# The first third of two units through the first layer during the last heads, and the denominator's product on GpSimd

## The chip, the core and the metric

The kernel runs on one core of one Trainium2 chip, as one launch. The metric is the device time in microseconds (us), taken as the median of several runs; a profile of one more execution comes with it. The engines are TensorE (PE, with its weight loads listed apart as PEld), VectorE (DVE), ScalarE (ACT) and GpSimd (POOL); SyncE (SP) issues the transfers.

## The reference

Three stages run one after the other, all in float32. The tensors q, k and v have 2 batches, 8 heads, 1152 rows and 64 columns.

```python
q_pool = q.reshape(B, H, S // 2, 2, D).mean(axis=3)
attn = softmax(q_pool @ k.T / sqrt(D)) @ v          # per head
x = attn as [1152 tokens, 512]

h = x @ w_in                                        # [1152, 2048]
P = a[0] + a[1]*h + a[2]*h**2 + a[3]*h**3
Q = 1.0 + abs(b[0])*abs(h) + abs(b[1])*h**2
x = (P / (Q + 1e-6)) @ w_out                        # [1152, 512]

xn = x / sqrt(mean(x*x) + 1e-6) * rms_g
out = (silu(xn @ w_gate) * (xn @ w_val)) @ w_out2   # width 1536
```

## The kernel before

**Work.** Every product of the two layers is three matmuls: activations and weights are kept as a high part and a low remainder, and high by high, high by low and low by high are summed in PSUM (`three`, line 507). Tokens are the columns, in NC = 3 thirds of CW = 384. A *unit* is 128 of the 2048 columns of the first layer, so there are 16 units; one unit takes 36 matmuls into its hidden tile `hid` (3 thirds, 4 slices kk of the 512 inputs, 3 products), and there are two such tiles in PSUM. Its function is computed from there, and 36 further matmuls take the result `g` into the sums `accp` of the second product, for a group of units at a time (GROUPS1 = 2, 4, 4, 4, 2).

**Attention.** 16 heads go in pairs, 9 tiles of 128 pooled rows to a pair, 72 tiles. Tiles are taken two by two: the scores (line 764), the row maximum `nm` on VectorE (793), the exponential `p` on ScalarE (799), the transposes on TensorE (815), their copies `pt` on ScalarE (847) or VectorE (850), and the product with v (`av`, 919). At the end of a pair of heads the copies `xt` are divided (970, 975) and split into x_hi and x_lo. The two score tiles are the same two PSUM tiles that the units use afterwards. Transposes of k, q and of the reciprocal sums (`rx`, 966) go through a PSUM tile of their own, `prep`. During attention the weights, which come as 64-bit numbers, are also decoded to float32 (`wc`) and split; what does not fit in SBUF goes to DRAM (`spill`, lines 211 to 232) and is fetched later. ScalarE, VectorE and GpSimd share that work.

**The function of a unit** (`rational`, line 1106 on, in `chain`). With u = m_u, p = m_p and q = m_q it is: u = |b1 h| (ACT 1106), p = a3 h + a2 (ACT 1109, all signs turned), p = p h (DVE 1112), p = (p + a1) h (DVE 1115), q = (u + b0) h (DVE 1122), q = |q| (ACT 1125), Ln and Exp of q for the reciprocal (ACT 1128, 1134), a correction factor from q and u (GpSimd 1140 after ACT 1131 for even units, DVE 1137 for odd ones), p = (p + a0) u (DVE 1143), g (DVE 1146), its high part (ACT 1154) and its low part (GpSimd 1157). Lines 1106, 1109, 1112, 1115 and 1122 read h from PSUM, and the hidden tile is free for the unit after next when they are done. Units 0 and 1 (FINE) do this third by third, the others for all tokens at once.

**Order.** Nothing is ordered by the engines. `Op` objects with an engine, a cost, a key and dependences are put in a list, and `order` sets each engine's queue once, while the program is built: of the operations that could start first by the costs, it takes the one with the smallest key. Some operations have several `ways`, that is engines, to choose from. What is written in the costs thus sets the order on the chip, and an engine works off its queue in that order, waiting where an input is not there. `order` runs once for attention (with `project_ops` of units 0 and 1 already in the list) and once for both layers.

## Time and profile before

| what | value |
|---|---|
| median of 3 runs | 723.6 us (721.89 to 726.38) |
| the profiled execution | 723.87 us |
| its span, first to last instruction | 722.0 us |
| mean granted TensorE clock | 0.986 of full speed |
| attention, until the first matmul of unit 0 | 265.15 us |
| busy: PE, DVE, ACT, POOL | 694.9, 542.4, 402.2, 299.7 us |

The times in the rows are counted from the start of the span. A row of a window gives the busy time of every engine in it, with the number of its instructions in brackets. A row of the chain gives start, length and work of a step of the path that ended last; "issue" there is time in which the profile shows nothing that the engine waited for. In a timeline, start and length of each instruction are followed by engine, line, and what it writes and reads.

### The profile page before, as it was taken

The page shows a single profiled execution, that of the slowest core. Times are in us where ns is not written, and L with a number is a line of the kernel's source. Part 1 is how long each engine was busy: PE and PEld are TensorE (multiplying, and loading weights), DVE is VectorE, ACT ScalarE, POOL GpSimd, SP SyncE. Part 2 cuts the span into 40 slices and gives each one's busy share as a digit, 9 for nine tenths or more (in the row PEclk, how much of TensorE's full clock was granted, in tenths as well). Part 3 has the DMA queues.
Part 4 walks back from the last instruction along what each step waited for, and adds up shares of the span by engine and source line. Part 5 has one row for each costly group of instructions (what it writes and reads, how often), then busy time and mean ns, then how long its engine had stood idle before and what let it go on. Part 6 is the DMA issues. An engine that isn't in the chain of part 4 may idle for free.

```text
span 722.0 us, 13129 instructions
## 1 busy us (share of the span) xinstructions
PE 694.9 (96%) x5257; PEld 605.0 (84%) x5257; DVE 542.4 (75%) x706; ACT 402.2 (56%) x620; POOL 299.7 (42%) x275
## 2 busy tenths in 40 slices
PE   7899999999999998899899999999999999999997
PEld 6677677767776777799899999998999899989996
DVE  4699988988888876887977879957769146945844
ACT  4668768778777767888755766435333223302210
POOL 4035546565655664424432343435345033513400
PEclk9999999999999999899999999999999999999999
DMA  6424536356554426114104104010223212420103
GB/s 208 118 76 150 154 99 216 128 186 220 167 183 162 145 108 233 59 59 145 59 30 146 59 0 147 26 35 0 88 88 119 87 58 70 136 88 29 59 1 131
DMA packets 51596, 77.13 MB, mean 107 GB/s; under 512 B 4176, under 2 KB 33872, under 8 KB 51536
## 3 DMA queue, kind: packets, MB, share of 16 engines
q1 hardware_dynamic: 51536, 76.30, 32.6%
q8 instruction: 41, 0.67, 0.4%
q14 instruction: 19, 0.16, 0.1%
HBM read 61.87 MB, written 14.42 MB: 106 GB/s over the span
## 4 chain that ended last, share of the span: by engine, by line
PE 88%; DVE 4%; ACT 4%; issue 1%; DMA 1%; SPq 0%; POOL 0%; POOLq 0%; DVEq 0%; ACTq 0%
PE hid L507 33%; PE accp L507 23%; PE hid L764 11%; PE av L919 10%; PE hid L815 7%; PE prep L712 3%; ACT p L799 2%; DVE nm L793 2%; ACT pt L847 1%; PE prep L966 1%; DMA wout_lo<-far 1%; DMA qn<-in_q_dram 1%; DVE win_lo L204 0%; ACT m_u L1106 0%; ACT m_q L1125 0%
## 5 line engine op out<-in xcount | busy, mean ns | idle before, releaser
L507 PE MATMUL hid<-x_hi,win_hi 128*128 128x384 f32 x480 | 162.7, 339 | 5.3 <-issue 2.8
L507 PE MATMUL hid<-x_lo,win_hi 128*128 128x384 f32 x480 | 161.8, 337 | 0.0
L507 PE MATMUL hid<-x_hi,win_lo 128*128 128x384 f32 x480 | 161.4, 336 | 0.0
L799 ACT ACTIVATE p<-hid,nm 128x1152 f32<-128x1152 f32 x72 | 88.0, 1222 | 36.8 <-DVE nm L793 36.6
L793 DVE TENSOR_REDUCE nm<-hid 128x1 f32<-128x1152 f32 x72 | 95.1, 1353 | 9.5 <-PE hid L764 8.8
L764 PE MATMUL hid<-kT,qT 64*128 64x256 f32 (+3 forms) x800 | 98.1, 379 | 0.6 <-ACT qT L598 0.2
L507 PEld LDWEIGHTS hid<-x_hi,win_hi 128*128 128x128 f32 x480 | 91.0, 190 | 8.0 <-issue 5.6
L507 PEld LDWEIGHTS hid<-x_lo,win_hi 128*128 128x128 f32 x480 | 91.0, 190 | 1.3 <-DVE x_lo L1315 0.3
L507 PEld LDWEIGHTS hid<-x_hi,win_lo 128*128 128x128 f32 x480 | 90.9, 189 | 0.0
L764 PEld LDWEIGHTS hid<-kT,qT 64*128 64x128 f32 (+1 forms) x800 | 73.6, 180 | 11.7 <-issue 1.6
L815 PEld LDWEIGHTS hid<-ident,p 64*128 64x128 f32 x1296 | 53.1, 141 | 33.5 <-ACT p L799 14.6
L919 PE MATMUL av<-pt,vn 128*64 128x288 f32 x576 | 76.7, 411 | 0.0
L815 PE MATMUL hid<-ident,p 64*128 64x64 f32 x1296 | 66.8, 231 | 9.0 <-ACT p L799 7.8
L1157 POOL TENSOR_TENSOR g_lo<-m_p,g_hi 128x1152 fp32r<-128x1152 f32 (+1 forms) x20 | 44.1, 2211 | 69.4 <-ACT g_hi L1154 69.4
L847 ACT ACTIVATE pt<-hid 128x512 f32<-128x512 f32 (+2 forms) x127 | 56.0, 477 | 25.3 <-PE hid L815 24.3
L507 PE MATMUL accp<-g_hi,wout_hi 128*128 128x384 f32 x192 | 66.0, 344 | 4.2 <-DVE acc L1212 2.0
L199 POOL TENSOR_SCALAR win_hi<-wc 128x512 fp32r<-128x512 f32 x26 | 18.2, 698 | 123.0 <-PE hid L507 104.1
L171 ACT ACTIVATE wc<-wraw 128x512 f32<-128x512 f32 x68 | 45.8, 675 | 41.7 <-POOL wout_lo L204 19.5
L850 DVE COPY pt<-hid 128x512 f32<-128x512 f32 (+2 forms) x97 | 50.9, 541 | 22.6 <-PE hid L815 21.1
L507 PE MATMUL accp<-g_lo,wout_hi 128*128 128x384 f32 x192 | 65.8, 343 | 0.6 <-POOL g_lo L1157 0.6
L507 PE MATMUL accp<-g_hi,wout_lo 128*128 128x384 f32 x192 | 65.7, 342 | 0.0
L919 PEld LDWEIGHTS av<-pt,vn 128*64 128x64 f32 x576 | 38.6, 136 | 26.9 <-issue 2.8
(118 smaller groups left out, 1276.0 us busy)
## 6 DMA issues: line engine op xcount, KB each, us to landing
wraw<-in_moe_w_out_dram SPq DMA_DIRECT2D x28, 512.0 KB, 3.4
far<-spill SPq DMA_DIRECT2D x23, 512.0 KB, 3.2
wraw<-in_moe_w_in_dram SPq DMA_DIRECT2D x16, 512.0 KB, 4.0
wraw<-in_moe_w_gate_dram SPq DMA_DIRECT2D x12, 512.0 KB, 3.6
wraw<-in_moe_w_val_dram SPq DMA_DIRECT2D x12, 512.0 KB, 3.7
kn<-in_k_dram SPq DMA_DIRECT2D x16, 288.0 KB, 3.7
vn<-in_v_dram SPq DMA_DIRECT2D x16, 288.0 KB, 3.4
qn<-in_q_dram SPq DMA_DIRECT2D x16, 256.0 KB, 3.4
```

The costliest lines, as they stand in the source:

```text
L171: nc.scalar.activation(c.bitcast(F32), wt["raw", n][:, :, 1].bitcast(F32), AF.Abs, scale=2.0**-112)
L199: eng.tensor_scalar(hi, w_float(n), 1.0, 1.0, op0=ALU.mult, op1=ALU.mult)
L507: ins = nc.tensor.matmul(dst, lhsT=a[x], rhs=b[y], start=first and i == 0 and p == 0, stop=last and i == n - 1 and p == 2,)
L712: seen(nc.tensor.transpose(ps[0:src.shape[1], at:at + 128], src, ident))
L764: ins = nc.tensor.matmul(ps[to, j, c:c + x1 - x0], lhsT=qT[2 * pr + h][rows, c0:c0 + to.stop - to.start], rhs=kT[2 * pr + h][rows, x0:x1], ...
L793: nc.vector.tensor_reduce(out=e["nm"], in_=scores(), op=ALU.max, axis=AX.X, negate=True)
L799: nc.scalar.activation(e["p"], scores(), AF.Exp, bias=e["nm"], scale=1.0, accum_out=sums[pr][:, t:t + 1])
L815: ins = nc.tensor.transpose(ps[:, g, c:c + 64], e["p"][rows, 128 * j:128 * j + 128], ident[rows, rows])
L847: return nc.scalar.activation(to, src, AF.Copy)
L850: return nc.vector.tensor_copy(to, src)
L919: nc.tensor.matmul(e["av", h][64 * c:64 * c + 64, 0:QW], lhsT=v_tile[2 * pr + h][:, KEYS[kt], :], rhs=pt[pr, h][:, kt, c * QW:(c + 1) * QW ...
L1157: eng.tensor_sub(g_(1), p_(), g_(0).bitcast(F32))
```

## The change

Two things are changed. First, for units 0 and 1 (PRE) the first third of the tokens, which belongs to the first batch and is ready long before the end of attention, is multiplied (12 matmuls a unit, into `prep`) and taken through the whole function while the last six of the 72 tiles run; the result stays in a new tile `pre`, and the buffers of k and of the pooled q serve as scratch. After attention only thirds 1 and 2 of these units are left, and `pre` is only split into its two parts. Secondly, for all 16 units the denominator is formed another way: ScalarE takes |h| without a factor, then w = b1 |h| + b0 (reading SBUF, in place of its |q|), and GpSimd multiplies w by |h|, in place of VectorE's line 1122. To make room, v has two buffers instead of three, and an unused constant goes.

```diff
     ON_POOL = range(0, 16, 2)
+    Q_POOL = range(16)
...
+        if w == "in" and u in PRE:
+            parts = [(c, kks) for c, kks in parts if c]
...
+    PRE = (0, 1)
+    def pre_ops(u, key, consts):
+        bps, bu, bq, bp = Buf("prep"), Buf("kn"), Buf("qp"), Buf("pre")
...
+        n = CW
+        mm = None
+        for kk in range(KC):
+            mm = Op(PE, cost(PE, 3 * n), key, lambda kk=kk: f_mm(kk), [mm or kq_mm[0], wop["in", u], *xop[0, kk]], [bps, *wbuf["in", u]])
+        o_abs = Op(ACT, cost(ACT, n), key + 2000, lambda: A(u_(), h_(), AF.Abs), [mm, *consts], [bps, bu])
+        o_p1 = Op(ACT, cost(ACT, n), key + 2000, lambda: A(p_(), h_(), AF.Identity, bias=na2, scale=na3), [mm, *consts], [bps, bp])
+        o_p2 = Op(DVE, cost(DVE, n), key + 2500, lambda: nc.vector.tensor_mul(p_(), p_(), h_()), [o_p1], [bps, bp])
+        o_p3 = Op(DVE, cost(DVE, n), key + 3000, lambda: stt(p_(), p_(), na1, h_(), op0=ALU.add, op1=ALU.mult), [o_p2], [bps, bp])
+        o_w = Op(ACT, cost(ACT, n), key + 3000, lambda: A(q_(), u_(), AF.Identity, bias=b0, scale=b1), [o_abs], [bu, bq])
+        o_q = op_any(
+            [(POOL, cost(POOL, n), lambda: f_q(nc.gpsimd)), (DVE, 1.2 * cost(DVE, n), lambda: f_q(nc.vector))],
+            key + 3500, [o_w], [bu, bq],
+        )
...
-        "kn": 2, "vn": 3, "qn0": 1, "qn1": 1, "qp": 2, "kT0": 1, "kT1": 1, "qT0": 1, "qT1": 1,
+        "kn": 2, "vn": 2, "qn0": 1, "qn1": 1, "qp": 2, "kT0": 1, "kT1": 1, "qT0": 1, "qT1": 1,
...
+    PRE_AT = 6
...
+    for u in PRE:
+        pre_ops(u, (NP * NT - PRE_AT + 2 * u) * TS, consts)
...
-                by_bank(A(as3(u_(), cs), h_(), AF.Abs, scale=b1))
+                by_bank(A(as3(u_(), cs), h_(), AF.Abs, scale=1.0 if u in Q_POOL else b1))
+
+            def f_w():
+                A(q_(), u_(), AF.Identity, bias=b0, scale=b1)
+
+            def f_qm(eng):
+                eng.tensor_mul(q_(), q_(), u_())
...
+            if u in PRE and cs == [0]:
+                bx = pre_buf[u]
+                o_hi = Op(
+                    ACT, cost(ACT, n), k + 5000, lambda: nc.scalar.activation(g_(0), pre_t[u], AF.Copy), [], [bx, *g]
+                )
...
-            o_q = Op(DVE, cost(DVE, n) + 60, k + 2000, f_q, [o_abs], [ps, bu, bq])
-            o_aq = Op(ACT, cost(ACT, n), k + 2000, f_aq, [o_q], [bq])
+            if u in Q_POOL:
+                o_w = Op(ACT, cost(ACT, n), k + 1500, f_w, [o_abs], [bu, bq])
+                o_aq = Op(POOL, cost(POOL, n), k + 2000, lambda: f_qm(nc.gpsimd), [o_w], [bu, bq])
+            else:
+                o_q = Op(DVE, cost(DVE, n) + 60, k + 2000, f_q, [o_abs], [ps, bu, bq])
+                o_aq = Op(ACT, cost(ACT, n), k + 2000, f_aq, [o_q], [bq])
```

The rest of the function in `pre_ops` (Ln, Exp, and the three last products on VectorE) is written as in `chain`.

TensorE's queue, from the scores of the tile that both heads of the last pair share: `prep<-ident,rx` are the reciprocal sums of the pair before, `av<-pt,vn` the product with v, `hid<-ident,p` the transposes. Before:

```order
L764 MATMUL hid<-kT_3386,qT_3429 64x128
L966 MATMUL prep<-ident,rx 128x128 x4
L919 MATMUL av<-pt,vn 64x288 x8
L815 MATMUL hid<-ident,p 128x64 x17
L952 MATMUL av<-ident,rx 128x128
L815 MATMUL hid<-ident,p 128x64 x18
```

and now, where `prep<-x,win` are unit 0's 12 matmuls (the first three stand here):

```order
L830 MATMUL hid<-kT_3382,qT_3425 64x128
L508 MATMUL prep<-x_hi,win_hi 128x384
L508 MATMUL prep<-x_lo,win_hi 128x384
L508 MATMUL prep<-x_hi,win_lo 128x384
...
L985 MATMUL av<-pt,vn 64x288 x8
L881 MATMUL hid<-ident,p 128x64 x34
L1018 MATMUL av<-ident,rx 128x128
L881 MATMUL hid<-ident,p 128x64
L830 MATMUL hid<-kT_3382,qT_3425 128x256 x4
```

Unit 0's 12 matmuls stand between the scores of one two-tile step and its transposes, and the reciprocal sums have moved behind them; unit 1's 12 stand in the next step, behind its transposes. After the last transposes 18 matmuls of unit 0 and, behind the last `av`, 18 of unit 1 come before the first that need the last pair of heads; before, these were 30 and 24.

GpSimd's queue at the end of attention, from the decoding of a weight on (`wc`, `spill`) over the last division `xt` to the first unit. Before:

```order
L215 TENSOR_TENSOR wc<-wc,wraw 128x512
L228 TENSOR_SCALAR spill<-wc 128x512
L232 TENSOR_TENSOR spill<-wc,spill 128x512
L975 TENSOR_TENSOR xt<-xt,rxh 64x64 x2
L1140 TENSOR_TENSOR m_q<-m_q,m_u 128x384 x3
L1157 TENSOR_TENSOR g_lo<-m_p,g_hi 128x384 x6
```

and now, where L1180 is the new product and L1214 the correction factor:

```order
L1041 TENSOR_TENSOR xt<-xt,rxh 64x64 x2
L213 TENSOR_TENSOR wc<-wc,wraw 128x512
L226 TENSOR_SCALAR spill<-wc 128x512
L230 TENSOR_TENSOR spill<-wc,spill 128x512
L1180 TENSOR_TENSOR m_q<-m_q,m_u 128x384 x2
L1214 TENSOR_TENSOR m_q<-m_q,m_u 128x384 x2
```

The last weight now stands behind the division, where VectorE at the same time makes x_hi and x_lo; it stood ahead of it.

VectorE's queue where unit 1 ends and unit 2 (the first with all 1152 tokens) begins, before:

```order
L1146 SCALAR_TENSOR_TENSOR m_p<-m_q,m_p 128x384 x3
L1122 SCALAR_TENSOR_TENSOR m_q<-m_u,absb,hid 128x1152
L1112 TENSOR_TENSOR m_p<-m_p,hid 128x1152
L1122 SCALAR_TENSOR_TENSOR m_q<-m_u,absb,hid 128x1152
L1115 SCALAR_TENSOR_TENSOR m_p<-m_p,ncoef,hid 128x1152
```

and now (1186 and 1189 are the old 1112 and 1115; 1217, 1211, 1220 the old 1143, 1137, 1146):

```order
L1186 TENSOR_TENSOR m_p<-m_p,hid 128x1152
L1217 SCALAR_TENSOR_TENSOR m_p<-m_p,ncoef,m_u 128x384 x2
L1211 SCALAR_TENSOR_TENSOR m_q<-m_q,m_u 128x384 x2
L1220 SCALAR_TENSOR_TENSOR m_p<-m_q,m_p 128x384 x2
L1189 SCALAR_TENSOR_TENSOR m_p<-m_p,ncoef,hid 128x1152
```

The last reader of unit 2's hidden tile (1115, now 1189) now stands behind unit 1's last six products, and the two denominators (1122) are gone.

## Rows read from the trace of the kernel before

**Rows 1.** The page's first part: busy us, share of the span, instructions.
```profile
PE 694.9 (96%) x5257; PEld 605.0 (84%) x5257; DVE 542.4 (75%) x706; ACT 402.2 (56%) x620; POOL 299.7 (42%) x275
```
**Rows 2.** Whom TensorE waited for, 250 to 480 us: total, times, longest.
```profile
PE hid L507 <- issue: 2.8, 2, 2.5
PE accp L507 <- DVE acc L1212: 2.0, 1, 2.0
PE hid L507 <- DVE m_p L1115: 1.9, 1, 1.9
PE accp L507 <- ACT g_hi L1154: 1.8, 1, 1.8
```
**Rows 3.** Windows: length, then PE, PEld, DVE, ACT, POOL busy, PE clock, transfers.
```profile
276.06:313.63 37.57, 32.49 (x158) 30.83 (x157) 31.40 (x45) 34.27 (x57) 14.85 (x14) 0.86 0.34 116
313.63:384.08 70.45, 67.94 (x392) 67.54 (x391) 58.41 (x50) 51.81 (x50) 27.94 (x10) 1.00 0.24 77
384.09:446.00 61.91, 61.91 (x360) 61.91 (x359) 51.02 (x45) 36.02 (x32) 20.65 (x9) 1.00 0.30 100
446.00:457.00 11.00, 8.95 (x43) 8.63 (x42) 10.37 (x12) 10.94 (x11) 5.01 (x3) 0.85 0.00 0
287.00:290.00 3.00, 3.00 (x11) 3.00 (x11) 2.10 (x4) 2.26 (x5) 2.56 (x3) 0.54 0.18 67
```
**Rows 4.** The chain that ended last, 256 to 400 us.
```profile
259.63 1.34 DVE nm L793
...
265.15 5.50 PE hid L507 x30
...
271.29 4.51 PE av L919 x36
...
276.06 4.70 PE hid L507 x27
...
284.07 1.06 DVE m_p L1115 x2
...
285.27 8.08 PE hid L507 x36
...
346.93 2.51 issue
...
384.09 12.48 PE hid L507 x72
```
**Rows 5.** Groups by shape: busy us, mean ns, idle before; ACT, DVE, POOL.
```profile
L1128 ACT ACTIVATE m_u<-m_q,b_lnq 128x384 f32<-128x384 f32 x6 | 3.5, 612 | 0.0
L1112 DVE TENSOR_TENSOR m_p<-m_p,hid 128x384 f32<-128x384 f32 x6 | 3.2, 546 | 0.0
L1122 DVE SCALAR_TENSOR_TENSOR m_q<-m_u,absb,hid 128x1152 f32<-128x1152 f32 x14 | 19.7, 1409 | 12.4 <-ACT m_p L1109 11.4 <-ACT m_u L1106 0.9
L1115 DVE SCALAR_TENSOR_TENSOR m_p<-m_p,ncoef,hid 128x1152 f32<-128x1152 f32 x14 | 19.7, 1409 | 0.1
L1143 DVE SCALAR_TENSOR_TENSOR m_p<-m_p,ncoef,m_u 128x1152 f32<-128x1152 f32 x14 | 24.6, 1757 | 2.5 <-ACT m_u L1134 2.4
L1157 POOL TENSOR_TENSOR g_lo<-m_p,g_hi 128x1152 fp32r<-128x1152 f32 x14 | 37.5, 2681 | 61.0 <-ACT g_hi L1154 61.0
L1140 POOL TENSOR_TENSOR m_q<-m_q,m_u 128x1152 f32<-128x1152 f32 x7 | 20.4, 2919 | 24.1 <-ACT m_q L1131 11.7 <-PE accp L507 7.7 <-issue 4.8
```
**Rows 6.** Timeline of DVE, then of POOL, around 340 us.
```profile
339.97 2.79 DVE L1143 SCALAR_TENSOR_TENSOR m_p<-m_p,ncoef,m_u 128x1152 f32<-128x1152 f32 x1 [0.75 <-ACT m_u L1134]
342.68 1.35 DVE L1137 SCALAR_TENSOR_TENSOR m_q<-m_q,m_u 128x1152 f32<-128x1152 f32 x1
...
338.87 2.68 POOL L1157 TENSOR_TENSOR g_lo<-m_p,g_hi 128x1152 fp32r<-128x1152 f32 x1 [5.12 <-ACT g_hi L1154]
```
**Rows 7.** Timeline of DVE, then of POOL: the last heads' x.
```profile
278.87 0.76 DVE L614 TENSOR_TENSOR x_lo<-xt,x_hi 128x576 fp32r<-128x576 f32 x1
...
276.38 1.30 POOL L232 TENSOR_TENSOR spill<-wc,spill 128x512 fp32r<-128x512 f32 x1
277.63 0.71 POOL L975 TENSOR_TENSOR xt<-xt,rxh 64x64 f32<-64x64 f32 x2
```
**Rows 8.** Timeline of DVE around 450 us, ahead of the late sums.
```profile
449.44 1.42 DVE L1122 SCALAR_TENSOR_TENSOR m_q<-m_u,absb,hid 128x1152 f32<-128x1152 f32 x1
450.77 1.42 DVE L1143 SCALAR_TENSOR_TENSOR m_p<-m_p,ncoef,m_u 128x1152 f32<-128x1152 f32 x1
452.10 1.01 DVE L1212 TENSOR_TENSOR acc<-acc,accp 128x384 f32<-128x384 f32 x2
```

More of the change, by code (lines that the diff above doesn't have):

```diff
@@ L551, in project, with h_, u_, q_ @@
         three([(env[w, u][:, c, 0:CW], pairs)], kks[0] == 0, kks[-1] == KC - 1, lambda ins: bank_access(w, u, c, ins))
+    PRE = (0, 1)
+    BUFS["pre"] = len(PRE)
+    pool("pre", len(PRE))
+    pre_t, pre_op = {}, {}
+    def pre_ops(u, key, consts):
+        bps, bu, bq, bp = Buf("prep"), Buf("kn"), Buf("qp"), Buf("pre")
+        e = {}
+        A = nc.scalar.activation
+        stt = nc.vector.scalar_tensor_tensor
+        def h_():
+            return e["h"][:, 0:CW]
+        def u_():
+            if "u" not in e:
+                e["u"] = T("kn", [128, NKT, D]).rearrange("p a d -> p (a d)")
+            return e["u"][:, 0:CW]
+        def q_():
+            if "q" not in e:
+                e["q"] = T("qp", [128, NQ, 2, D]).rearrange("p a r d -> p (a r d)")
+            return e["q"][:, 0:CW]
+        def p_():
+            if u not in pre_t:
+                pre_t[u] = T("pre", [128, CW])
+            return pre_t[u]
+        def f_mm(kk):
+            if kk == 0:
+                e["h"] = T("prep", [128, 512], F32, space=PSUM)
+            wx = weight("in", u)
+            three([(h_(), [([t[:, kk, :] for t in wx], [t[:, kk, CS[0]] for t in (x_hi, x_lo)])])], kk == 0, kk == KC - 1)
+        def f_q(eng):
+            eng.tensor_mul(q_(), q_(), u_())
[12 more added lines that the diff above has]
+        )
+        o_ln = Op(ACT, cost(ACT, n), key + 4000, lambda: A(u_(), q_(), AF.Ln, bias=b_lnq, scale=2.0**-62), [o_q], [bu, bq])
+        o_exp = Op(ACT, cost(ACT, n), key + 4500, lambda: A(u_(), u_(), AF.Exp, bias=b_expq, scale=-1.0), [o_ln], [bu])
+        o_m = Op(DVE, 1.2 * cost(DVE, n), key + 5000, lambda: stt(q_(), q_(), 1.0 + 1e-6, u_(), op0=ALU.add, op1=ALU.mult), [o_exp], [bu, bq])
+        o_t = Op(DVE, 1.2 * cost(DVE, n), key + 5000, lambda: stt(p_(), p_(), na0, u_(), op0=ALU.add, op1=ALU.mult), [o_exp, o_p3], [bu, bp])
+        pre_op[u] = Op(
+            DVE, 1.2 * cost(DVE, n), key + 5500,
+            lambda: stt(p_(), q_(), 2.0, p_(), op0=ALU.subtract, op1=ALU.mult), [o_m, o_t], [bq, bp],
+        )
+        pre_buf[u] = bp
@@ L554, in attention_moe_moe2_kernel @@
+    pre_buf = {}
     inner = ExitStack()
@@ L1032, in attention_moe_moe2_kernel @@
     consts = Op("SP", 1450, 20000, load_consts, [later])
-    Op(DVE, 80, 60000, negate_coef, [consts])
-    Op(ACT, 80, 60000, abs_b, [consts])
+    consts = [Op(DVE, 80, 60000, negate_coef, [consts]), Op(ACT, 80, 60000, abs_b, [consts])]
     for n in range(AHEAD):
@@ L1179, in chain @@
             env["table"] = o_exp
-        for cs in [[c] for c in range(NC)] if u in FINE else [list(range(NC))]:
+        for cs in [[c] for c in range(NC)] if u in FINE or u in PRE else [list(range(NC))]:
             chain(cs)
```

11 lines of the change are left out of this document (9 added, 2 removed).

## The prediction

> **What bounds the kernel now.** The page's first part comes first: TensorE is busy 96% of the span and the next engine, VectorE, 75% [rows 1]. So TensorE's own matmuls set the time, and a change that adds and removes none can only win where TensorE stands or runs at the lower clock. Second come the windows, which say where that is. In a full stretch 72 matmuls of the chain take 12.48 us, 0.1733 us each [rows 4]. Taking that as the price, each window's length less its count times 0.1733 is what was lost in it [rows 3]: 37.57 − 158 × 0.1733 = 10.2 us at the change from attention to layer one, 70.45 − 392 × 0.1733 = 2.5 us in the units after it, 11.0 − 43 × 0.1733 = 3.5 us at the late sums; the window of 61.91 us between has a clock of 1.00 and TensorE busy throughout. Together 16.2 us, the most the change could give: 723.9 − 16.2 = 707.7.
>
> Third, who is late there. The waits of 250 to 480 us name VectorE's 1115 (the last reader of a hidden tile), VectorE's copies `acc` and ScalarE's `g_hi`, each about 2 us, and 2.8 us of "issue" [rows 2]. The longest of the last, 2.51 us at 346.93, lies in the second window [rows 2 to 4]: it is TensorE before the hidden tile whose last reader is the 1115 of two units before, late because VectorE lost time at 340 us [rows 6]. Part of the first window's loss is not a wait at all: 36 matmuls from 285.27 took 8.08 us in place of 6.24 [rows 4], with a granted clock of 0.54 at 287 to 290 us, the lower level of 1.2 GHz [rows 3], after TensorE had waited for 1115 at 284.07 [rows 4]. I put that 1.8 us on each such stop.
>
> **The change part by part.** No matmul is added; 24 are moved. The sum goes against the profiled 723.87 us, which stands 0.3 above the median.
>
> *Attention's end, TensorE.* When the last `av` ends, before at 271.29 + 4.51 = 275.80 us [rows 4], 24 + 18 matmuls of units 0 and 1 are now done where 30 were: 12 more, 12 × 0.1733 = 2.08 us. What of that falls in time in which TensorE would stand is gain. The chain shows it behind a row maximum of 1.34 us at 259.63 [rows 4]; I take 0.8 of the 2.08 as hidden there and let the end of `av` slip by 1.3, to 277.1. Ends: +2.1, and the loss of the slow rival below.
>
> *Attention's end, VectorE and ScalarE.* Both units together add ten operations of 384 columns to each engine, at 0.55 us (1112) on VectorE and 0.61 at most on ScalarE [rows 5]: 5.5 and 6 us. VectorE also takes the split of the last pair. The last six of the 72 tiles, at 265.15 / 72 = 3.7 us each [rows 4], last 22 us, of which VectorE is idle some 25% by the mean share [rows 1], 5.5 us. They just fit; I cost them at nothing beyond the 1.3.
>
> *The last pair's x.* Before, x_lo ended at 278.87 + 0.76 = 279.63, 3.8 us behind `av` [rows 7], and 24 matmuls (4.2 us) covered it. Now 18 (3.1 us) do: 0.7 missing. GpSimd's last spill no longer stands ahead of the division (it ended at 277.68 [rows 7]), but runs beside x_lo. That GpSimd holds up VectorE is shown at 340 us: 1143, which reads two operands in SBUF, took 2.79 us while GpSimd's 1157 ran from 338.87 to 341.55, against 1.35 for the like operation right behind it [rows 6]. x_lo reads two such operands; half of a 1.30 us operation [rows 7] makes another 0.6. TensorE waits 1.3 here, between 0 and 2.
>
> *Units 2 to 4.* The tile of unit 2 waits for unit 0's two thirds instead of three, and these start six matmuls further on: 0.5 us left of the wait that ended at 285.27. Unit 3's waits for unit 1's thirds, behind two denominators on GpSimd of some 1 us (2.92 / 3 [rows 5]): 1.3. For unit 4 the change is worse than before: its tile waits for unit 2's 1115, which now stands behind the last six products of unit 1, 6 × 0.55 = 3.3 us [rows 5], and these wait for GpSimd's product, ScalarE's Ln and Exp. Nothing of the trace shows this queue. If everything were ready in time it costs nothing, since TensorE has 36 + 12 matmuls (8.3 us) for unit 3 and the sums; if unit 1's third is late by one GpSimd operation and one chain of Ln and Exp (1.0 + 2 × 0.61), with the 3.3 behind it, some 5 us. I take 2.4, the middle. With one clock drop of 1.8 and 0.5 to fill, the window loses 1.3 + 0.5 + 1.3 + 2.4 + 1.8 + 0.5 = 7.8 in place of 10.2. With the 0.8: **3.2 us gained**, between −2 and 8.
>
> *Each full unit.* VectorE loses 1122, 1.41 us [rows 5]. ScalarE stays as it was, with w for |q|. GpSimd takes 2.92 by the row of the same operation, 1140 [rows 5]: with 1157 and every second 1140, 2.92 + 2.68 + 1.46 = 7.06 us a unit. In the window at full clock a unit is 72 matmuls, 12.5 us, and GpSimd goes from 33% [rows 3] to 56%: it fits. In the run of units without sums, of 36 matmuls (6.2 us) and a few more, it doesn't, and works from a stock. The detour lengthens a unit's chain by 2.92 − 1.41 = 1.5 us and by a wait for 1157 of the unit before. It also holds up VectorE's operations with two SBUF operands: 1143 has a mean of 1.76 against 1.41 for 1115, which reads PSUM [rows 5], 0.35 each at 33%; at 56%, 0.59 for each of the 2.5 operations of a unit, 0.6 more a unit. That leaves VectorE 1.41 − 0.6 = 0.8 us better off, and 1115 comes earlier by up to 1.4. Of the 2.5 us of the second window I take 1.3 to stay: **1.2 us gained**, from −5 (GpSimd late, below) to 2.5.
>
> The Trainium skill speaks against this step: "GPSIMD Engine Reference", section "4.1 Engine selection", has elementwise two-operand work on VectorE, as about twice as slow on GpSimd. The trace agrees, 2.92 against 1.41, and by the page's factor alone the step loses 1.4 us a unit; it counts only where a unit's chain is what TensorE waits for.
>
> *The late sums.* At 449.44 VectorE did a 1122 and then a 1143, 2.8 us, before the copies `acc` for which TensorE stood 2.0 us [rows 2, 8]. In the new order neither stands ahead of those copies, and a shorter stop also spares the clock (0.85 in this window [rows 3]). Of 3.5 us 0.3 is left: **3.2 us gained**, between 1 and 3.5. The norm and the second layer keep their order: nothing. v with two buffers has its transfers shifted by one place; its tiles are loaded more than a pair of heads ahead of use, so nothing, and about 1 us if that cover were gone.
>
> Sum: 3.2 + 1.2 + 3.2 = 7.6; 723.9 − 7.6 = 716.3, and as a median **716.0 us**.
>
> **The rivals.** *The waits vanish.* If unit 4's tile and the last x are ready in time and no clock drop remains, the first window loses 2 instead of 7.8 and the second 0.5: 716.0 − 5.8 − 0.8 = 709.4, so 707.5 to 713. For it: VectorE, which the waits name most [rows 2], gets lighter in every unit. Against it: its queue at unit 2.
>
> *GpSimd becomes what is waited for.* A product queued behind 1157 and beside VectorE's reads delays Ln, Exp and g. Unit 4's tile then costs 5.0 in place of 2.4, and in the run of units without sums, where GpSimd needs 7.06 us of some 7.3 a unit, the last g comes one product and one 1157 later (2.92 + 2.68), of which 1 is slack: 4.6 more. 716.0 + 2.6 + 4.6 = 723.2, so 719 to 724. For it: 1143's 2.79 us [rows 6]. The Trainium skill makes this a rule: by "SBUF — State Buffer", section "Who interferes with whom", a VectorE instruction with two SBUF inputs contends with a GpSimd instruction that reads SBUF, over one shared port. The trace agrees with its 2.79 against 1.35. Against it: the time between a unit's h and the use of its g is a whole group of units for most units.
>
> *Slower: the new operations hold up the last heads.* The 5.5 us on VectorE stand ahead of row maxima on which scores, exponentials and transposes hang; of the six among them that read two SBUF operands, two to four may each wait for a whole GpSimd operation of 1.30 us [rows 7] (GpSimd is busy 42% [rows 1]), which makes 8.1 or 10.7. It decides from the point at which they exceed the 5.5 us of idle time above: then each further microsecond goes on the path. If all of 8.1 does, with one more clock drop of 1.8 and the start's gain lost, the time is 723.6 − 1.2 − 3.2 + 8.1 + 1.8 = 729.1; with 10.7, 731.7. For it: the chain runs through nm [rows 4]. Against it: VectorE's mean of 75% is over the whole span, and its decoding of weights can move to other engines.
>
> That the change doesn't do what it says is no case: the order shows both parts in their places.
>
> **How the numbers follow.** About 1% (7.2 us, so 716.4 and 730.8) is what a measurement of this kernel can tell from no change. Forecast, 713 to 719: 0.50, of which 0.28 lies below 716.4. Waits vanish, 707.5 to 713: 0.22. GpSimd, 719 to 724: 0.18. Slower, 727 to 734: 0.10, of which 0.07 is above 730.8. So faster 0.50, same 0.43, slower 0.07. Leaving out the slow case (0.10), the top of GpSimd's (0.06) and the lowest of the good one (0.04) gives 708.5 to 722.5.
>
> **What the profile would show.** Right: last `av` at about 277 us; a wait for x_lo near 280 of 1 to 2 us; TensorE's waits for unit 4's tile below 3 us with one stretch at the lower clock; late sums without a stop of 2 us on `acc`; GpSimd's new product near 2.9 us and VectorE's 1217 at 1.9 to 2.1. It is wrong if `av` ends beyond 280 us, if TensorE waits over 5 us for unit 4 or for a `g`, or if the new product takes over 3.5 us beside VectorE's reads.

## The result, and the profile after

The changed kernel takes 733.8 us (median of 6 runs, 731.21 to 736.8) against 723.8 for the kernel before: 1.0148 times as long, 95% interval 1.0125 to 1.017, so it is 1.5% slower. The forecast of 716.0 and its range, which ended at 722.5, are both missed. The profiled execution has a span of 733.9 us and a time of 735.65.

The page's first part, against [rows 1]:

```profile
PE 697.5 (95%) x5257; PEld 604.4 (82%) x5257; DVE 547.9 (75%) x691; ACT 402.0 (55%) x620; POOL 345.6 (47%) x288
```

VectorE has lost its 20 instructions of the old line 1122, has 15 fewer in all, and is busy 5.5 us longer. GpSimd took over 45.5 us of products, and its busy time rose by 45.9. TensorE's work is the same 5257 matmuls. So the place to look is VectorE, and then where TensorE paid for it. The waits of TensorE from 250 to 480 us, as in [rows 2]:

```profile
PE hid L508 <- issue: 9.9, 3, 4.9
PE accp L508 <- DVE acc L1304: 7.3, 7, 1.6
PE hid L508 <- DVE x_lo L680: 1.3, 1, 1.3
PE hid L508 <- DVE m_p L1189: 0.5, 1, 0.5
```

Before, "issue" and `acc` were 2.8 and 2.0 us; now they are 9.9 and 7.3. The waits for x_lo and for unit 0's last reader are small. To see when the time was lost I number the 1152 matmuls of layer one in TensorE's order. Their count is the same in both kernels, so the start of the n-th can be compared (from the timeline of TensorE; 0.1733 us each is the floor):

| n-th matmul of layer one | before, us | after, us | later by |
|---|---|---|---|
| 54 | 280.06 | 279.94 | -0.1 |
| 200 | 315.91 | 314.42 | -1.5 |
| 300 | 333.24 | 333.79 | 0.6 |
| 400 | 353.39 | 359.10 | 5.7 |
| 500 | 370.76 | 378.10 | 7.3 |
| 1000 | 461.34 | 473.24 | 11.9 |
| 1151 | 489.22 | 501.34 | 12.1 |

The heads and the first units are no slower: at the 200th matmul the changed kernel is ahead. All of the loss comes behind, most of it between the 300th and the 500th (the tiles of units 6 to 9; the tile of unit 7 waits for the function of unit 5). Behind layer one the difference stays at 12. What became slower there is seen in the groups of VectorE and GpSimd by shape, from 276 to 500 us (1217, 1220, 1211 are the old 1143, 1146, 1137):

```profile
L1220 DVE SCALAR_TENSOR_TENSOR m_p<-m_q,m_p 128x1152 f32<-128x1152 f32 x14 | 32.4, 2315 | 0.2 <-POOL m_q L1214 0.2
L1217 DVE SCALAR_TENSOR_TENSOR m_p<-m_p,ncoef,m_u 128x1152 f32<-128x1152 f32 x14 | 29.4, 2103 | 5.0 <-ACT m_u L1208 4.9
L1189 DVE SCALAR_TENSOR_TENSOR m_p<-m_p,ncoef,hid 128x1152 f32<-128x1152 f32 x14 | 19.7, 1409 | 1.8 <-ACT m_u L1174 1.6
...
L1180 POOL TENSOR_TENSOR m_q<-m_q,m_u 128x1152 f32<-128x1152 f32 x14 | 41.2, 2945 | 10.3 <-ACT m_q L1177 10.3
L1231 POOL TENSOR_TENSOR g_lo<-m_p,g_hi 128x1152 fp32r<-128x1152 f32 x14 | 40.2, 2869 | 25.6 <-ACT g_hi L1228 25.6
```

and of the kernel before, in the same window, the old 1220:

```profile
L1146 DVE SCALAR_TENSOR_TENSOR m_p<-m_q,m_p 128x1152 f32<-128x1152 f32 x14 | 18.9, 1353 | 4.3 <-POOL m_q L1140 4.2
```

1189, which reads one operand from PSUM, takes the same 1.409 us as in [rows 5]. 1217 and 1220, which read two from SBUF, take 2.10 and 2.32 us; 1143 took 1.76 [rows 5], and 1146 1.35. One such stop, in the timelines of VectorE, GpSimd and TensorE:

```profile
335.52 3.06 DVE L184 SCALAR_TENSOR_TENSOR wc<-wraw,wc 128x512 uint32<-128x512 uint32 x1
338.50 3.81 DVE L1220 SCALAR_TENSOR_TENSOR m_p<-m_q,m_p 128x1152 f32<-128x1152 f32 x1
342.23 1.34 DVE L1186 TENSOR_TENSOR m_p<-m_p,hid 128x1152 f32<-128x1152 f32 x1
343.61 1.41 DVE L1189 SCALAR_TENSOR_TENSOR m_p<-m_p,ncoef,hid 128x1152 f32<-128x1152 f32 x1
...
334.88 3.14 POOL L1231 TENSOR_TENSOR g_lo<-m_p,g_hi 128x1152 fp32r<-128x1152 f32 x1
337.99 3.10 POOL L1180 TENSOR_TENSOR m_q<-m_q,m_u 128x1152 f32<-128x1152 f32 x1
...
345.12 0.66 PE L508 MATMUL hid<-x_hi,win_hi 128*128 128x384 f32 x1 [4.93 <-issue]
```

GpSimd's new product runs until 341.09. VectorE's 1220, issued half a microsecond behind its start, ends 1.2 us after it, about its whole own length. The last reader of the hidden tile (1189) stands behind 1220 in VectorE's queue and ends at 345.02, and TensorE, which has stood for 4.93 us, goes on at 345.12. The product held VectorE, and not the unit whose product it was but the one ahead of it paid. Not all of the stop is the product's: just ahead of 1220 a weight's decoding (line 184), which took 0.69 us at 462.50, took 3.06 beside the low part 1231.

I call the time above the usual length (1.36 us, 0.58 for a third) of VectorE's operations with two SBUF operands in the function of layer one (1217, 1211, 1220, and the old lines for them) *hold*, summed over those that are over 0.2 us longer; the decoding of weights is not in it. By single operations it is 8.3 us before and 30.1 after; 15.7 of the 30.1 lie behind the new product, 7.2 behind the low part 1231 and 7.2 behind the correction 1214. VectorE lost 23.4 us of work (1122) and got 21.8 us more hold. (The expectations below use sums in which a timeline row of two or three thirds counted as one long operation: 12.3, 32.1 and 16.1 us for 8.3, 30.1 and 15.7, and 12.1 for 10.1 in that of e15. Every sum of hold in the text is by single operations.)

### The profile page after: what moved, and what is told of

It is laid out like the page before. It is cut to its first block, busy times and chain, and to the rows that moved or that the text cites. A ratio compares the mean times of both kernels' runs of the same rounds, so it can differ in the third digit from the quotient of the medians.

```text
span 733.9 us, 13129 instructions
## 1 busy us (share of the span) xinstructions
PE 697.5 (95%) x5257; PEld 604.4 (82%) x5257; DVE 547.9 (75%) x691; ACT 402.0 (55%) x620; POOL 345.6 (47%) x288
## 4 chain that ended last, share of the span: by engine, by line
PE 76%; DVE 11%; ACT 6%; issue 4%; POOL 2%; DMA 0%; SPq 0%; DVEq 0%; POOLq 0%; ACTq 0%
PE hid L508 29%; PE accp L508 17%; PE hid L830 11%; PE av L985 9%; PE hid L881 6%; PE prep L778 3%; DVE m_p L1220 2%; DVE m_p L1217 2%; DVE nm L859 1%; ACT p L865 1%; DVE acc L1304 1%; ACT m_p L1183 1%; ACT pt L913 1%; ACT g_hi L1228 1%; DVE m_q L1211 1%
## 5 line engine op out<-in xcount | busy, mean ns | idle before, releaser
L913 ACT ACTIVATE pt<-hid 128x512 f32<-128x512 f32 (+2 forms) x128 | 56.0, 474 | 26.6 <-PE hid L881 25.5
L169 ACT ACTIVATE wc<-wraw 128x512 f32<-128x512 f32 x68 | 45.9, 676 | 39.8 <-POOL wout_lo L202 19.6
L508 PE MATMUL accp<-g_lo,wout_hi 128*128 128x384 f32 x192 | 64.2, 335 | 0.0
```

The lines of the kernel that those rows point to most:

```text
L169: nc.scalar.activation(c.bitcast(F32), wt["raw", n][:, :, 1].bitcast(F32), AF.Abs, scale=2.0**-112)
L508: ins = nc.tensor.matmul(dst, lhsT=a[x], rhs=b[y], start=first and i == 0 and p == 0, stop=last and i == n - 1 and p == 2,)
L913: return nc.scalar.activation(to, src, AF.Copy)
```

## Experiments

Theory P: GpSimd's reads hold VectorE. Theory L: the detour over GpSimd makes a unit's chain longer, whoever holds whom. Theory H: the inserted operations hold up the last heads. After the second group a fourth was added, S: the reads of both engines share one path, and its whole occupation counts, not only VectorE's standing. The median of the kernel before was 723.1 to 724.0 in the groups; ratios are against it. Edits that only change what a function issues (e4 to e9, e12, e16, e17) leave the order of every queue as it was; the others have their order planned anew.

**The two parts apart, and the product elsewhere.** First, only the first part (e1):

```diff
-    Q_POOL = range(16)
+    Q_POOL = ()
```

> Only the first part of the change: the first thirds of units 0 and 1 go ahead during the last heads, the denominators of all units stay as before on VectorE. In the trace of the changed kernel the 200th matmul of layer one starts 1.5 us earlier than before, and the 1000th 11.9 us later, so the loss of 12.1 us arises behind the first units. Theory P (the product on GpSimd reads SBUF and holds up VectorE's operations with two SBUF operands: the mean of the last product, L1220, went from 1.35 to 2.31 us) and theory L (the detour over GpSimd's queue makes each unit's chain longer, whoever holds whom) both expect a gain: 1.5 us and up to 4 of the waits at units 3 and 4 that the product caused, so 717 to 722. Theory H (the last heads pay for the ten inserted operations) expects 730 to 735.

Measured: 726.2 us, 1.0033 (1.0019 to 1.0047). The time lies in neither range. H is out as the cause of the loss of 10 us, but so is the gain that I expected. Only the second part (e2):

```diff
-    PRE = (0, 1)
-    BUFS["pre"] = len(PRE)
-    pool("pre", len(PRE))
+    PRE = ()
```

> Only the second part: GpSimd makes the denominator's product for all units, nothing goes ahead during the heads (v keeps two buffers). Theories P and L: the loss without the first part's gain, 733 to 738. Theory H: 720 to 724.

Measured: 734.7 us, 1.0155 (1.0138 to 1.0172). The loss belongs to the second part. It lies in the full units here too: this kernel was 5.7 us ahead of the kernel before at the 200th matmul (310.21) and 10.6 behind at the 1151st (499.85). The product on VectorE (e3):

```diff
-                o_aq = Op(POOL, cost(POOL, n), ..., lambda: f_qm(nc.gpsimd), [o_w], [bu, bq])
+                o_aq = Op(DVE, cost(DVE, n) + 60, ..., lambda: f_qm(nc.vector), [o_w], [bu, bq])
```

> Both parts, with the new form (ScalarE makes w from SBUF), but the product w |h| on VectorE with two SBUF operands instead of on GpSimd. Theories P and L: nothing of the product is left on GpSimd, VectorE has the 1.35 us that the old line 1122 took, so about the time of the first part alone, 716 to 722, with the mean of the last product of a unit (L1220) back under 1.6 us. Rival F (the new form itself, whoever multiplies, delays the units, since |q| was one operation later in the old chain): 728 to 734.

Measured: 729.6 us, 1.008 (1.0059 to 1.0101): in the range of F, against P and L. The trace shows another reason than F's: the product with two SBUF operands now was itself held, 1.85 us in the mean, where the old 1122 with h from PSUM had 1.41 [rows 5]. F as such is answered by e5 below, which has the new form and a detour as long, and takes 724.7. The old form was the better one on VectorE, too.

**Writes instead of reads, in the same order.** This tells P from L, since every queue and wait stays (e4):

```diff
             def f_qm(eng):
-                eng.tensor_mul(q_(), q_(), u_())
+                eng.memset(q_(), 1.0)
+                eng.memset(q_(), 1.0)
```

> The changed kernel with its order, but at the product's place GpSimd writes 1.0 into the tile twice and reads nothing; the denominators are left out of the computation. The place in every queue and all waits stay; GpSimd still stands in the chain for the length of two writes (not known, 2 to 3 us together if one is half of the product's 2.95). Theory P: without GpSimd's reads VectorE isn't held, L1220 falls from 2.31 to 1.4 to 1.7 us (what 1231 and 1214 still hold) and the time to 718 to 724. Theory L: with two writes of 2 us or more in the chain it stays at 730 to 734.

Measured: 722.3 us, 0.9973 (0.9945 to 1.0002), as P. The two writes took only 2.14 us, so L wasn't out. With a third one (e5):

> As the kernel that writes 1.0 twice in place of GpSimd's product (there the two writes took 2.14 us, shorter than the product's 2.95, so the shorter chain could have been the gain of 11.5 us), but with three writes, 3.2 us: the chain is now longer than with the product, and GpSimd reads nothing; the denominators are left out of the computation. Theory P (GpSimd's reads hold VectorE's operations with two SBUF operands): 721 to 726, since nothing is held by the writes. Theory L (the length of the detour): 733 to 737.

Measured: 724.7 us, 1.0004 (0.9979 to 1.0028). The groups of this kernel by shape:

```profile
L1180 POOL MEMSET m_q<- 128x1152 f32 x14 | 14.9, 1066 | 9.0 <-ACT m_q L1177 9.0
L1181 POOL MEMSET m_q<- 128x1152 f32 x14 | 15.0, 1073 | 0.8
L1182 POOL MEMSET m_q<- 128x1152 f32 x14 | 15.2, 1085 | 0.8
...
L1222 DVE SCALAR_TENSOR_TENSOR m_p<-m_q,m_p 128x1152 f32<-128x1152 f32 x14 | 28.7, 2050 | 2.1 <-POOL m_q L1216 2.0
L1219 DVE SCALAR_TENSOR_TENSOR m_p<-m_p,ncoef,m_u 128x1152 f32<-128x1152 f32 x14 | 19.8, 1412 | 5.7 <-ACT m_u L1210 5.6
```

The detour is 3.2 us, longer than the product's 2.95, and 9 us of the 10 are gone: L is out as the main cause. One more microsecond of detour a unit cost some 2.4 us (724.7 against 722.3), which is not clear of noise, as their intervals overlap. Line 1219 (the 1217 above) is back at 1.41 us from 2.10. Line 1222 (the 1220) is not, at 2.05 from 2.32, and e4's expectation of 1.4 to 1.7 is missed with 1.97: of the 12.1 us of hold that are left 9.7 lie there, in front of them all a read of GpSimd that stayed (low part, correction, or once a weight's split). Not one operation is held behind a write. So it is the reading, not GpSimd's being busy, that holds VectorE. (By the Trainium skill, "SBUF — State Buffer", section "Who interferes with whom", VectorE's second SBUF operand contends with a GpSimd instruction that reads SBUF and not with one that only writes it; these runs agree.)

**Short pieces.** If a hold lasts for one GpSimd instruction, three short ones should do less harm than a long one (e6):

```diff
-                eng.tensor_mul(q_(), q_(), u_())
+                for i in range(len(cs)):
+                    s = CS[i]
+                    eng.tensor_mul(q_()[:, s], q_()[:, s], u_()[:, s])
```

> The changed kernel in its order, with GpSimd's product of a whole unit split into three instructions of 384 columns, about 1.0 us each, so the product takes as long as before. Theory P, if a hold lasts for one instruction: a VectorE operation waits 1 us at most behind the product; of 32.1 us of holds in layer one, 16.1 stood behind the product, 8 to 10 of them go, and at 0.8 us of time for each us of hold (11.5 us for 14.7 between the changed kernel and the one with two writes) the time is 725 to 729. Theory P2 (a held operation stands until GpSimd is done with all three, since they follow without a gap): 732 to 735. Theory L: 733 to 736.

Measured: 731.1 us, 1.01 (1.007 to 1.0131), with 21.3 us of hold, outside every range. Then all three of GpSimd's operations of a unit in thirds, by the same loop in the two others (e7):

> As the run with the split product, and GpSimd's other two operations of a unit (the correction factor and the low part of g) are split into thirds too. Theory P: all holds are 1 us at most, the 32.1 us fall to 12 to 16 and the time to 718 to 724. Theory P2: 731 to 736. Theory L: 733 to 737.

Measured: 733.1 us, 1.0135 (1.0074 to 1.0196), and P in its simple form fails: the hold is halved, 13.7 us, and the time is that of the changed kernel. (P2 and L had this time, but P2 expected the hold to stay, and L fell with e5.) GpSimd's groups show what came in its place:

```profile
L1182 POOL TENSOR_TENSOR m_q<-m_q,m_u 128x384 f32<-128x384 f32 x46 | 58.5, 1296 | 13.1 <-ACT m_q L1177 13.1
L1237 POOL TENSOR_TENSOR g_lo<-m_p,g_hi 128x384 fp32r<-128x384 f32 x46 | 52.3, 1163 | 15.5 <-ACT g_hi L1232 15.5
```

A third of the product takes 1.30 us, so a unit's product 3.9 instead of 2.95. In the timelines of this kernel it is seen that VectorE now holds GpSimd:

```profile
399.20 2.97 POOL L1182 TENSOR_TENSOR m_q<-m_q,m_u 128x384 f32<-128x384 f32 x3 [3.84 <-ACT m_q L1177]
...
419.89 4.60 POOL L1182 TENSOR_TENSOR m_q<-m_q,m_u 128x384 f32<-128x384 f32 x3 [2.11 <-ACT m_q L1177]
...
420.92 1.71 DVE L1213 SCALAR_TENSOR_TENSOR m_q<-m_q,m_u 128x1152 f32<-128x1152 f32 x1
423.88 1.82 DVE L1224 SCALAR_TENSOR_TENSOR m_p<-m_q,m_p 128x1152 f32<-128x1152 f32 x1
```

Alone (VectorE then reads h from PSUM) the three take 2.97 us; beside 1213 and 1224 they take 4.60. What VectorE doesn't lose, GpSimd does: its operations of the function are, by the same kind of sum (above 2.66 us, 1.00 for a third), 9.2 us too long in the changed kernel and 22.7 us in this one. A unit's chain waits for both. This is theory S. The same split of its two operations in the kernel before (e8):

> The kernel before, without either part of the change, with the two operations that GpSimd does in a unit split into thirds. It had 12.3 us of holds in layer one. Theory P: 4 to 6 us of them stay, and the time falls by 0.2 to 0.8 us for each us that goes, 717 to 722. Theory P2 and L: 722 to 725.

Measured: 720.2 us, 0.9939 (0.9914 to 0.9965): a gain of 3.6 us, in P's range. It lies at the late sums, where TensorE's wait for `acc` fell from 2.0 us to 0.4: 1.3 us behind the kernel before at the 500th matmul, 1.9 ahead at the 1000th. The hold hardly fell (7.1 from 8.3 us), and S, by which nothing changes with the same reads in shorter pieces, does not explain it.

**The path's occupation.** By S it shouldn't matter which of GpSimd's reads goes. The product is kept and the low part of g is replaced by writes (e9):

```diff
             def f_lo(eng=nc.gpsimd):
-                eng.tensor_sub(g_(1), p_(), g_(0).bitcast(F32))
+                if eng is nc.gpsimd:
+                    eng.memset(g_(1).bitcast(F32), 0.0)
+                    eng.memset(g_(1).bitcast(F32), 0.0)
+                else:
+                    eng.tensor_sub(g_(1), p_(), g_(0).bitcast(F32))
```

> The changed kernel in its order with GpSimd's product kept, but GpSimd's other large operation, the low part of g (L1231), replaced by two writes of zeros (2.1 us together), so that the low part of g is left out of the second product. Theory S (the reads of GpSimd and the two-operand reads of VectorE share one path, and its total occupation counts: a unit needs 2.68 + 2.92 + 1.46 us of GpSimd and 2.5 x 1.36 us of VectorE, 10.5 us, in the changed kernel, 7.5 us before and with writes in place of the product): here 7.8 us, so about the time of before, 723 to 727, though the product stands where it stood. Theory P (what counts is VectorE standing behind the product itself): only the 7.2 us of holds behind 1231 go, 727 to 731. Theory L (the detour's length): 732 to 735.

Measured: 724.4 us, 0.9999 (0.9977 to 1.0021). But these writes didn't wait for g's high part, so the run was repeated with one column that does (e16):

```diff
...
+                    f = slice(0, 1)
+                    eng.tensor_sub(g_(1)[:, f], p_()[:, f], g_(0).bitcast(F32)[:, f])
+                    eng.memset(g_(1).bitcast(F32)[:, 1:], 0.0)
+                    eng.memset(g_(1).bitcast(F32)[:, 1:], 0.0)
...
```

> As the run with the product kept and two writes of zeros at the place of g's low part (724.4), but there the writes didn't wait for g's high part, so a unit's chain was also shorter at its end. Now GpSimd first makes one column of the low part (and so waits for the high part), then writes the other 1151 columns twice, some 2.3 us against 2.7; those columns of the low part are left out of the computation. Theory S: 7.8 us of demand, 723 to 727. Theory P: 727 to 731. If the shorter end of the chain made the earlier gain: 731 to 734.

Measured: 725.0 us, 1.0012 (0.9987 to 1.0037), with the product where it was in every queue. Both times lie in S's range and not in P's or that of the shorter chain. The same pair on the kernel before, both of GpSimd's operations as writes, without (e12) and with (e17) that column; the low part is edited as in e9 and e16, the correction so:

```diff
             def f_m_pool():
-                nc.gpsimd.tensor_mul(q_(), q_(), u_())
+                nc.gpsimd.memset(q_(), 1.0)
+                nc.gpsimd.memset(q_(), 1.0)
```

> The kernel before in its order, with both GpSimd operations of a unit (the correction factor and the low part of g) replaced by two writes each, 2.1 us in place of 2.9 and 2.7; both are left out of the computation. Theory S: the path's demand falls from 7.5 to 3.4 us a unit and no VectorE operation is held; if it bounds layer one already before the change, the time falls to 713 to 719. If TensorE's order and ScalarE bound it, 720 to 723.

> As the kernel before with writes at the places of GpSimd's two operations (717.2), but with one column of g's low part made first, so that it waits for the high part as in the kernel before; the rest of the low part and the correction factor of the even units are left out of the computation. Theory S (holds of 12.3 us are gone and GpSimd isn't held either): 715 to 719. If the shorter end of the chain made the gain: 721 to 724.

Measured: 717.2 us, 0.992 (0.989 to 0.995), and 718.3 us, 0.9937 (0.9914 to 0.9959). No operation of the function is held in either. So the reads cost the kernel before some 5.7 us already, with what the shorter length of the writes (0.3 to 0.8 us an operation) gave, which no run separates. The opposite of the change, the correction factor of every unit on VectorE (e13):

```diff
-    ON_POOL = range(0, 16, 2)
+    ON_POOL = ()
```

> The kernel before, without either part of the change, with the correction factor of all units on VectorE (before: even units on GpSimd, 2.92 us, odd ones on VectorE, 1.36 us), so a change in the opposite direction to the one studied: work with two SBUF operands goes from GpSimd to VectorE. Theory S: demand on the shared path 6.7 in place of 7.5 us a unit, 719 to 723. VectorE as the bound (0.7 us a unit more work, 75% busy): 725 to 729.

Measured: 720.2 us, 0.9954 (0.9935 to 0.9973): more work on VectorE, and 3.8 us faster. This order is planned anew, and the gain was there (4.4 us) at the 200th matmul; so S's range is met, but the order is a rival that this run doesn't exclude. The product on GpSimd only outside units 5 to 9 (e10):

```diff
-    Q_POOL = range(16)
+    Q_POOL = [0, 1, 2, 3, 4, 10, 11, 12, 13, 14, 15]
```

> Both parts of the change, but units 5 to 9, which TensorE takes with few sums between them (some 7 us a unit), keep their denominators on VectorE; the other 11 units have GpSimd's product. Between the 300th and the 500th matmul of layer one, where these units lie, the changed kernel lost 6.8 us against the one before, and 4.5 us behind. Theory R (the path is over-full only in that run, 10.5 us of demand against some 7 us of TensorE): the 6.8 us go, 725 to 728. Theory S without place (each product costs the same wherever it is, 11/16 of the loss stays): 729 to 732.

Measured: 731.3 us, 1.0118 (1.0083 to 1.0152): as S without place. Between the 300th and the 500th matmul it still lost 4.6 us more than before (42.12 against 37.52).

The runs in the order of the path's occupation a unit, worked out as in the expectations (2.68, 2.92 and 1.46 us of GpSimd's reads, 1.36 for each of VectorE's two-operand reads):

| kernel | occupation, us a unit | hold, us | median, us |
|---|---|---|---|
| before, writes for both (e12) | 3.4 | 0.0 | 717.2 |
| the same, waiting for the high part (e17) | 3.4 | 0.0 | 718.3 |
| before, corrections on VectorE (e13) | 6.8 | 6.3 | 720.2 |
| the same, low part in thirds (e19) | 6.8 | 4.9 | 719.5 |
| the same with the first part (e18) | 6.8 | 6.3 | 723.8 |
| before | 7.5 | 8.3 | 723.1 to 724.0 |
| before, both in thirds (e8) | 7.5 | 7.1 | 720.2 |
| first part alone (e1) | 7.5 | 9.1 | 726.2 |
| the same, last weight first (e11) | 7.5 | 10.1 | 725.0 |
| the same, both in thirds (e15) | 7.5 | 7.3 | 719.7 |
| changed, two writes for the product (e4) | 7.5 | 15.5 | 722.3 |
| changed, three writes for the product (e5) | 7.5 | 12.1 | 724.7 |
| changed, low part of g as writes (e9) | 7.8 | 22.9 | 724.4 |
| the same, waiting for the high part (e16) | 7.8 | 18.4 | 725.0 |
| changed, product on VectorE (e3) | 8.9 | 16.1 | 729.6 |
| changed, product outside units 5 to 9 (e10) | 9.5 | 23.5 | 731.3 |
| changed, product in thirds (e6) | 10.5 | 21.3 | 731.1 |
| changed, all in thirds (e7) | 10.5 | 13.7 | 733.1 |
| changed | 10.5 | 30.1 | 733.8 |
| second part alone (e2) | 10.5 | 25.1 | 734.7 |

From group to group the time follows the second column: 717 to 718 us at 3.4, 719 to 726 at 6.8 to 7.8, 730 to 731 at 8.9 to 9.5, 731 to 735 at 10.5. Within a group it does not: at 7.5 the times are 6.5 us apart. The third column orders most of them too, but not e7 (13.7 us of hold and 733.1) nor e9 and e16 (22.9 and 18.4, and 724 to 725). So the sum is a rough measure, and that its size sets the time is argued from this order, not shown.

**The first part.** Alone it was 1.9 us ahead of the kernel before at the 200th matmul and 2.8 us behind at the 1000th. One loss lay at the start, in the timelines of VectorE and of SyncE's queue of the first part alone:

```profile
282.87 2.52 DVE L1240 TENSOR_TENSOR g_lo<-pre,g_hi 128x384 fp32r<-128x384 f32 x2
288.30 0.61 DVE L1196 SCALAR_TENSOR_TENSOR m_q<-m_u,absb,hid 128x384 f32<-128x384 f32 x1 [2.92 <-issue]
...
285.00 0.32 SPq L235 DMA_DIRECT2D far<-spill  x1
```

The last weight now stands behind the division, and its transfer to DRAM was issued at 285.00. All such transfers of this kernel took:

```profile
DMA to landing us min/median/max: 2.6/3.4/4.8
```

So it landed at 287.6 at the earliest; the trace has the landing at 287.93, and VectorE's wait for that queue, ahead of 1196, ending at 287.96. The first write to a tile `m_q` (1196, the old 1122) waits for DMA queues, which it did not before; it came at 288.30, and TensorE waited 4.4 us for unit 0's last reader. The changed kernel has the same stop, on ScalarE, whose w (1177) is its first write to an `m_q`; there the transfer was issued at 285.24:

```profile
288.35 1.31 ACT L1177 ACTIVATE m_q<-m_u,absb 128x384 f32<-128x384 f32 x2 [2.46 <-issue]
```

To move that weight back, the division was made to wait for it (e11, with the first part alone):

```diff
         spill_ops(n, NP * NT * TS + 8000 * n)
+    [o for o in ops if o.cost == 566][-1].deps.append(wop["spill", s_lo])
```

> The first part of the change alone, and the last weight of the heads is put to DRAM before the last division, as in the kernel before. With the first part alone the time was 726.2, and unit 2's tile came 4.6 us late, because the first write to a tile of layer one waited for the transfer of that last weight out of SBUF (288.3 us; unit 0's h was there at 283.7). Theory A (the start's gain is lost there): that wait falls to some 2 us, and the time to 722 to 724. Theory G (whatever is won at the start is given back in the run of units 5 to 9, where the function of a unit takes VectorE and ScalarE longer than its matmuls take TensorE): the start is 2 us better by the 200th matmul, the end stays within 1 us of 726.

Measured: 725.0 us, 1.0024 (1.0007 to 1.004). The 4.4 us became 0.6 (and x_hi came 1.4 us late instead), and the 200th matmul came 3.3 us before that of the kernel before; by the 500th it was 1.2 us behind it. That is G. VectorE's window of the first part alone goes with it:

```profile
335.00:368.00 33.00, 28.74 (x152) 27.52 (x151) 32.35 (x24) 23.47 (x21) 11.92 (x6) 0.95 0.14 49
```

VectorE is busy 32.35 of 33 us where these units lie (98%; in the kernel before 23.72 of 26 us from 334 us on, 91%), and TensorE comes sooner only to wait longer. With GpSimd's two operations in thirds as well (e15):

> The first part of the change alone, with the last weight ahead of the last division (725.0), and GpSimd's two operations of a unit split into thirds (which in the kernel before gave 720.2 in place of 723.8). If the two add: 721 to 722. Theory G (the start's gain, 3 us by the 200th matmul, is given back in the run of units 5 to 9 because VectorE stands there behind GpSimd; of 12.1 us of holds 6 to 9 lie there): with short holds the start's gain stays, 717 to 720. If the split moves the waiting to GpSimd in that run: 723 to 726.

Measured: 719.7 us, 0.9948 (0.9931 to 0.9966), against 720.2 for the split without the first part: the start's 1.6 us at the 200th matmul were 0.4 at the 500th and nothing at the 1151st. The time is in G's range, but the gain is the split's, and that of the start did not stay. Lastly both reliefs, the thirds and the corrections on VectorE, with (e18) and without (e19) the first part:

> Three changes together: the first part (first thirds ahead, last weight before the last division), g's low part on GpSimd in thirds, and the correction factor of all units on VectorE. Theory S: demand on the shared path 6.7 us a unit in short pieces; the corrections on VectorE gave 3.8 us alone, the thirds 3.6, the first part nothing beside them: 715 to 719. Theory G: not below the same without the first part (e19). If VectorE, with the corrections and the first thirds, becomes the bound of the units without sums: 720 to 724.

> The kernel before with two changes: g's low part on GpSimd in thirds, and the correction factor of all units on VectorE. Theory S: 715 to 719, if the two gains (3.6 and 3.8) come from different places; 719 to 721 if both came from the same stop at the late sums.

Measured: 723.8 us, 1.0003 (0.9982 to 1.0024), and 719.5 us, 0.9949 (0.9931 to 0.9967). S's range, 715 to 719, is missed by e18 and, narrowly, by e19. The reliefs don't add up: in both of these a wait of 3.8 to 3.9 us stands before the 378th matmul (2.5 in the kernel before). And e19's time is the one expected if both gains came from the stop at the late sums, but that stop, which the thirds had taken away in e8, is still 1.7 us long there. With the first part 4.3 us are lost again, the outcome expected if VectorE becomes the bound; that it did wasn't shown by a further run. Four versions (e8, e13, e15, e19) are faster than both kernels (than the one before by 0.5 to 0.6%); the plainest is the kernel before with GpSimd's two operations in thirds.

## Why the prediction was wrong

**What bounds the kernel** held: TensorE's matmuls are the same, and all of the difference arises within layer one, in waits and, for some 2.6 us, in slower matmuls (TensorE is busy 697.5 us against 694.9).

**Attention's end** held in its numbers. `av` ended at 277.75 us (277.1 forecast), TensorE waited 1.3 us for x_lo (1.3) and 0.5 for unit 2's tile (0.5). That the 1.3 fits is in part luck: the last weight had left its place ahead of the division, but the weight before it stood there instead, and x_hi waited 1.07 us for the division behind it:

```profile
278.65 1.61 POOL L230 TENSOR_TENSOR spill<-wc,spill 128x512 fp32r<-128x512 f32 x1
280.22 0.71 POOL L1041 TENSOR_TENSOR xt<-xt,rxh 64x64 f32<-64x64 f32 x2
...
280.97 0.46 DVE L667 TENSOR_SCALAR x_hi<-xt 128x576 fp32r<-128x576 f32 x1 [1.07 <-POOL xt L1041]
```

The slow rival, which had the right size (727 to 734), named the wrong place: the heads lose nothing, and e1 shows it.

**Units 2 to 4** were right in sum only at first. Unit 3's tile came 3.4 us late in place of 1.3, with the last 1189 of unit 1 behind two thirds of 1220 that had waited for GpSimd. Ahead of those stand the 2.46 us in which w waited for the transfer of the last weight (285.9 to 288.35), for which I had put nothing. And the 36 matmuls of unit 3 took 9.04 us, with a granted clock of 0.50 for 5.3 us (the lower level, 1.2 GHz), in place of 6.24 plus a drop of 1.8:

```profile
297.91:303.20 5.29, 5.29 (x17) 5.29 (x18) 3.46 (x6) 5.29 (x10) 2.75 (x4) 0.50 0.01 3
```

Unit 4's tile, for which I had put 2.4 and up to 5, was not waited for. Of the 3.2 us forecast, 1.5 were there at the 200th matmul, and none at the 300th.

**Each full unit** is the step that failed. I had the mechanism and its sign (VectorE's operations with two SBUF operands stand still behind GpSimd), but scaled the mean hold of 1143 with GpSimd's busy share: 0.35 to 0.59 us an operation, 0.6 more a unit, against 1.41 saved. Measured: 19.6 us more hold over the 14 full units (26.6 against 7.0), 1.4 a unit, all that 1122 had freed. The busy share was the wrong measure, because the product isn't spread evenly. It starts when ScalarE has made w, and as at 338 us this is often when VectorE reaches the last products of the unit ahead; 1146, which had cost 1.35 us and in no full unit had been held, became the operation most held (2.32). And the hold didn't stay on VectorE: in its queue 1189 and the copies `acc` stand behind 1217 and 1220, so both hidden tiles and sums came late. The forecast gain of 1.2 us became 6.8 lost between the 300th and the 500th matmul. My signs for this step were the wrong ones: the new product (2.95 in the mean) and 1217 (2.10) came as forecast, and 1220 I had not looked at.

**The late sums** failed with it. 1122 no longer stands ahead of those copies, but a 1217 of 3.64 us does, at 468.28:

```profile
468.28 3.64 DVE L1217 SCALAR_TENSOR_TENSOR m_p<-m_p,ncoef,m_u 128x1152 f32<-128x1152 f32 x1
471.84 0.54 DVE L1304 TENSOR_TENSOR acc<-acc,accp 128x384 f32<-128x384 f32 x1
...
468.03 2.68 POOL L1214 TENSOR_TENSOR m_q<-m_q,m_u 128x1152 f32<-128x1152 f32 x1 [0.43 <-ACT m_q L1205]
```

TensorE waited 4.5 us for `acc` from 440 to 480 us, in four stops of at most 1.6, where it had waited 2.0 in one [rows 2]. From the 500th to the 1000th matmul 4.6 us were lost in place of 3.2 won.

**The rivals.** "GpSimd becomes what is waited for" had the cause, by its argument from 1143's 2.79 us [rows 6], and the rule of the Trainium skill that I set beside it spoke for it. Its price, 7.2 us above the forecast, was 17.8: I priced two places, unit 4's tile and the last g, and it acts in every unit. The objection that I held against it, that there is a whole group of units between h and g, is about g; the late things were hidden tiles and sums.

What stays open: why the product outside units 5 to 9 (e10) still lost 4.6 us inside them, why shorter pieces help the kernel before (e8) and not the changed one (e7), and why the two reliefs didn't add up; the orders of e10, e18 and e19 were planned anew, and no run kept them fixed.

## What to carry to other kernels

Moving work from the second busiest engine to an idle one gained nothing here, because the two then held each other up: count the two-operand SBUF reads of VectorE and GpSimd's reads together, per unit of work, before counting each engine's busy time, and take the sum as a warning, not as a time. Operations that read one operand from PSUM were outside this sum (1.41 us in the changed kernel as before), so an operation that does is the last one to move. And what an earlier start won (3.3 us in e11) was gone at the end, behind a stretch in which VectorE was busy 98% (window of e1).

## What the runs showed of the hardware

The exclusion works both ways: VectorE's held operation ended 1.2 us after GpSimd's, about its whole own length of 1.35, as if it had begun only then, though the trace shows it as running for 3.81 us and not as waiting; and a third of GpSimd's product grew from 0.99 us (2.97 for three, alone) to 1.53 (4.60 for three) beside VectorE's reads. I had not expected the splitting to move the loss from one engine to the other without changing the time. GpSimd's write of 1152 columns took 1.07 us against 2.95 for the product, and behind 42 of them no operation of VectorE was held.
